# Earlier choice of slots and another order of loads for the first expert, in a kernel of linear attention and a mixture of experts

## The chip, the cores and the metric

The kernel runs on one core of one Trainium2 chip. The time is the device time of one execution in microseconds; several executions are timed and the median counts. A profile is taken of one further execution.

## The reference

The attention part keeps a 40 x 40 state for each of 4 x 8 heads and steps through 768 positions. Its output is the input of a mixture of 8 experts, of which each token uses the one with the largest logit.

```python
for t in range(S):                       # attention, B=4, H=8, S=768, D=40
    y[:, :, t] = einsum('bhd,bhde->bhe', rt, state)
    Sa = einsum('bhde,bhe->bhd', state, at)
    state = state * wt[:, :, None, :] - einsum('bhd,bhe->bhde', Sa, bt) \
            + einsum('bhd,bhe->bhde', vt, kt)
...
x = attn_out.transpose(0, 2, 1, 3).reshape(B * S, H * D)      # 3072 x 320
logits = x @ w_gate                      # experts, E=8, D=320, F=1024
e_idx = argmax(logits, axis=1)
...
for e in range(E):
    h = maximum(x[mask] @ w1[e], 0.0)
    out[mask] = gate_w[mask, None] * eom[mask, e, None] * (h @ w2[e])
```

## The kernel before

**Attention.** The positions are cut into 12 chunks of 64. In each chunk a triangular system has to be solved for 32 heads, 16 in each half (q = 0 and 1). `Att.run` writes out the order by hand as coroutines that yield after each step. A background coroutine prepares chunks (`prep`: loads, scans, masks on POOL, products pl on PE) and inverts the triangles of two chunks at once on DVE (`tinv`, with the tiles Tt, Ns, tmpf, and as its last step the transpose of line 350 into Tc). The chain from chunk to chunk is `crit`: five steps for each half, with matmuls into pa, evictions As on ACT (line 399), the copies XU (lines 438 and 439), and the state's step pS, tmS and XS. After each step of `crit` the background goes on by four steps (`RATE = 4`). `tail` computes the output of a half (VU, pM, the masked products M on DVE, pY) and ends in x on DVE (line 495), which `route` transposes (pxt) and multiplies by the gates into logits LG. When all inversions are written out, the pool of the preparation's tiles closes (`s.pre.close()`) and the background runs `Moe.early`; its pools stand on the other side of SBUF and take over this memory.

**Choice of slots.** `pick` takes the logits of several chunks at a time, as `NB` says: after chunk 3 chunks 0 to 3, after chunk 7 chunks 4 to 7, after chunk 10 chunks 8 to 10, after chunk 11 this one. It runs 18 small instructions on DVE, finds each token's place in its expert, and writes records into a table `tab` in DRAM with one indirect DMA from POOL for each half chunk (line 739), each of which waits for the one before. After chunk 7 (`HALF`) the first 240 places of each expert are all that the early work uses.

**The first expert.** `early` loads the weights of expert 0 through one staging tile st (4 KB a partition): three pieces of w1, three of w2. Each is loaded on SP's queue, cast on ACT to a rounded part (w1h, w2h; lines 767 and 774), and subtracted on DVE for the rest (w1l, w2l; lines 769 and 775). `slots` reads the table into tr (line 846) and turns it on DVE into tb (line 848) and ti (line 850); `tokens` gathers 240 tokens with two indirect DMAs (line 789) and transposes them into xh and xl. `expert` then computes eight blocks of the first layer (ph, line 820; 8 matmuls each here, then hh on ACT and hl on DVE), of which `early` runs the first `E0 = 4` inside the attention, and the second layer (po, lines 833 to 835), whose rows go out by indirect DMA. `experts` runs what is left when the attention's memory is free, beginning with the loads of expert 1.

The instructions of each engine are put in order by a planner, from the order in which they are written, their dependencies and its own estimate of durations. `issue_after(i)` keeps what is written under it behind instruction i on the engine of i.

Of the kernel before, what the change touches and what calls it, by code (L numbers as in the profile page):

```python
# [9 lines left out]
F32 = mybir.dt.float32  # L10
F32R = mybir.dt.float32r
# [4 lines left out]
ALU = mybir.AluOpType  # L16
# [578 lines left out]
E0 = 4  # L595


class Moe:
    def __init__(s, ctx, tc, ident, wg, wo, w1, w2, out):
        s.tc, s.nc, s.ident = tc, tc.nc, ident  # L600
# [50 lines left out]
        s.nc.sync.dma_start(out=s.tab.rearrange("(p n) f -> p n f", p=128), in_=s.t0)  # L651

    HALF, HT, half = 7, 2, False
    NB = {3: (0, 4), 7: (4, 4), 10: (8, 3), 11: (11, 1)}

    def route(s, c, q, x, pool, psx):

# [91 lines left out]
        V.tensor_reduce(out=out, in_=t, axis=AX.X, op=ALU.max)  # L749


    def weights(s, e, wp, sp):

        nc = s.nc
        w1h = wp.tile([128, 3, FF], F32R, name="w1h", tag="w1h")
        w1l = wp.tile([128, 2, FF], F32R, name="w1l", tag="w1l")
        w2h = wp.tile([128, 8, DM], F32R, name="w2h", tag="w2h")
        w2l = wp.tile([128, 8, DM], F32R, name="w2l", tag="w2l")
# [83 lines left out]
    def slots(s, pool):  # L842

        nc = s.nc
        tr = pool.tile([TS, 32, 4], F32, name="tr", tag="tr")
        nc.sync.dma_start(out=tr, in_=s.tab.rearrange("(t p) f -> p t f", p=TS))
        tb = pool.tile([TS, 4, 32], F32, name="tb", tag="tb")
        nc.vector.tensor_copy(out=tb, in_=tr.rearrange("p t f -> p f t"))
        ti = pool.tile([TS, 2, 32], I32, name="ti", tag="ti")
        nc.vector.tensor_copy(out=ti, in_=tb[:, 0:2])  # L850
        return tb, ti

    def early(s, ctx, psx):

        pool = lambda n, b: ctx.enter_context(s.tc.tile_pool(name=n, bufs=b, side="right"))
        s.wpa, s.tp0 = pool("wpa", 1), pool("tp0", 1)
        with s.tc.tile_pool(name="sp0", bufs=1, side="right") as sp:
            w = s.weights(0, s.wpa, sp)
            s.W0 = next(w)
            yield from w  # L860
        while not s.half:
            yield
        s.tabs = s.slots(s.tp0)
        t = s.tokens(s.tabs, 0, 0, 2, s.tp0, psx)
        T = next(t)
        next(t)
        for _ in range(30):
            yield
        yield from t
        s.hp0 = ExitStack()  # L870
        hp = s.hp0.enter_context(s.tc.tile_pool(name="hp0", bufs=E0, side="right"))
        s.hp = hp, TS * 2
        s.E0 = s.expert(2, s.W0, T, lambda: s.hp, lambda: s.ps1(), lambda: s.ps2())
        s.ps1 = lambda: psx(CAP)
        for _ in range(E0):
            next(s.E0)
            yield

    def experts(s, ctx):
        tc = s.tc  # L880
# [9 lines left out]
        def tok(tabs, *u):  # L890
            t = s.tokens(tabs, *u, tp, psx)
            T[u[:2]] = next(t)
            next(t)
            return t

        def wts(e):
            w = s.weights(e, s.wpa if e % 2 == 0 else wpb, sp)
            W[e] = next(w)
            return w

# [4 lines left out]
            for _ in prep:  # L905
                pass

        t = tok(s.tabs, 1, 0, 2)
        w = wts(1)
        tabs = s.slots(tp)  # L910
        t2 = tok(tabs, 0, 2, 2)
        unit(0, 0, 2, chain(w, t))
        s.hp0.close()
# [131 lines left out]
def rwkv_moe_kernel(tc, win, din, rl, vl, vt, r, k, v, w, a, b, wg, wo, w1, w2, out, nch=12):  # L1045
    nc = tc.nc
    with ExitStack() as ctx:
# [6 lines left out]
        with ExitStack() as c1:  # L1054
            with ExitStack() as c2:
                att = Att(c2, tc, ident, win, din, rl, vl, vt, nch=nch)
                moe.fill()
                ps = lambda sh, nm, tag="tl", n=3: lambda *_: att.ps.tile(sh, F32, name=nm, tag=tag, bufs=n)
                att.run(lambda c, q, x: moe.route(c, q, x, att.p2, ps([128, 4, 128], "pxt")),
                        moe.loads, lambda: moe.early(c1, lambda n: ps([128, 512], "px0", "pl", 2)()[:, 0:n]))  # L1060
# [45 lines left out]
```

## Time and profile before

| | us |
|---|---|
| median of 3 runs | 725.73 |
| lowest and highest run | 725.46, 727.76 |
| the profiled execution | 727.63 |
| its span in the profile | 725.9 |
| PE busy | 648.0 (89%) |
| DVE busy | 465.7 (64%) |
| ACT busy | 344.8 (47%) |
| POOL busy | 206.8 (28%) |

The span is the time between the first and the last instruction that the profile shows. The busy time is summed over the span. All times in the rows below count from the start of the span. PE is the matmul engine TensorE, DVE is VectorE, ACT is ScalarE, POOL is GpSimd, SP the engine that issues most DMAs.

### The profile page before, as it was taken

The numbers are of one execution on the slowest core, as the hardware profiler recorded it, in microseconds if no ns is written. First come the engines' busy times: TensorE is split into PE (matmuls) and PEld (weight loads), VectorE is DVE, ScalarE is ACT, GpSimd is POOL, SyncE is SP. The second block draws the span as 40 slices with busy tenths as digits, with TensorE's granted clock in tenths as the row PEclk, the third lists the DMA queues.
The fourth block names the chain that finished last, engine by engine and source line by source line (L and its number), as shares of the span: only waits on it lengthen the run. The fifth ranks groups of instructions, "written<-read, shape, count | busy, mean of one in ns | idle before, by whom it ended". The sixth has DMA issues, their size and how long they took to land.

```text
span 725.9 us, 21141 instructions
## 1 busy us (share of the span) xinstructions
PE 648.0 (89%) x8866; PEld 582.8 (80%) x8866; DVE 465.7 (64%) x904; ACT 344.8 (47%) x791; POOL 206.8 (28%) x316
## 2 busy tenths in 40 slices
PE   6766887899998899989999898779999999999993
PEld 6655776788887787887888788679999998898993
DVE  7694699648997994899289554353675445544230
ACT  4866642376387237835753354142563334333120
POOL 9632302123134036304112100334433142412111
PEclk9867998799998899999999989889999999999997
DMA  8785443157556365652325742085575433530000
GB/s 200 170 191 139 117 121 78 55 140 176 121 135 149 90 109 126 144 123 80 98 61 103 139 122 78 21 229 143 151 220 160 125 117 105 183 89 24 25 12 22
DMA packets 66007, 85.12 MB, mean 117 GB/s; under 512 B 34766, under 2 KB 51793, under 8 KB 65906
## 3 DMA queue, kind: packets, MB, share of 16 engines
q1 hardware_dynamic: 61976, 74.67, 41.6%
q0 software_dynamic: 3840, 8.91, 4.3%
q8 instruction: 72, 1.18, 0.7%
q14 instruction: 29, 0.24, 0.1%
q10 hardware_dynamic: 90, 0.13, 0.1%
HBM read 67.59 MB, written 8.96 MB: 105 GB/s over the span
## 4 chain that ended last, share of the span: by engine, by line
PE 49%; DVE 16%; issue 12%; DMA 10%; ACT 8%; POOL 1%; SPq 1%; POOLq 0%; ACTq 0%; DVEq 0%
PE ph L820 12%; PE pa L408 5%; PE po L835 4%; PE po L833 4%; PE po L834 4%; PE pM L480 4%; ACT N L250 4%; DVE tmpf L328 3%; PE pl L242 3%; PE pt L184 2%; DMA out_dram<-y,ti 2%; PE pY L493 2%; ACT LA L230 2%; PE pY L492 2%; PE pS L446 2%
## 5 line engine op out<-in xcount | busy, mean ns | idle before, releaser
L825 DVE SCALAR_TENSOR_TENSOR hl<-ph,hh 128x480 fp32r<-128x480 f32 (+1 forms) x76 | 41.9, 563 | 67.0 <-ACT hh L824 54.5
L820 PE MATMUL ph<-xh,w1h 128*128 128x480 f32 (+1 forms) x228 | 79.8, 354 | 2.5 <-DVE hl L825 1.3
L833 PE MATMUL po<-w2h,hh 128*120 128x320 f32 x256 | 79.0, 312 | 1.9 <-ACT hh L824 1.7
L820 PE MATMUL ph<-xl,w1h 128*128 128x480 f32 (+1 forms) x228 | 79.4, 351 | 0.0
L232 POOL TENSOR_SCALAR_AFFINE_SELECT LA<-LA 64x192 f32<-64x192 f32 x144 | 57.1, 428 | 75.1 <-ACT LA L230 73.9
L824 ACT ACTIVATE hh<-ph 128x480 fp32r<-128x480 f32 (+1 forms) x76 | 36.8, 497 | 87.3 <-PE ph L820 81.6
L834 PE MATMUL po<-w2l,hh 128*120 128x320 f32 x256 | 78.0, 308 | 0.0
L835 PE MATMUL po<-w2h,hl 128*120 128x320 f32 x256 | 75.7, 310 | 0.0
L838 POOL DMA_INDIRECT out_dram<-y,ti x32 | 33.7, 1054 | 139.7 <-DVE y L837 74.0
L242 PE MATMUL pl<-Am,kb 120*128 120x192 f32 (+1 forms) x288 | 63.3, 357 | 9.8 <-DMA Am<-Av 5.6
L399 ACT ACTIVATE As<-pa,hq 128x320 f32<-128x320 f32 x80 | 41.8, 528 | 54.6 <-PE pa L408 34.2
L250 ACT ACTIVATE N<-pl 32x384 f32<-32x384 f32 (+1 forms) x144 | 54.2, 376 | 23.8 <-PE pl L242 11.3
L739 POOL DMA_INDIRECT tab<-rec,si x24 | 27.7, 1153 | 119.4 <-DMA tab<-rec,si 48.3
L242 PEld LDWEIGHTS pl<-Am,kb 120*128 120x128 f32 x288 | 48.6, 212 | 13.6 <-ACT LA L230 5.2
L480 PE MATMUL pM<-R,VU 128*128 128x128 f32 x384 | 55.4, 300 | 3.6 <-ACT VU L472 3.5
L493 PE MATMUL pY<-KB,M 128*64 128x40 f32 x768 | 54.3, 230 | 1.0 <-DVE M L484 0.7
L480 PEld LDWEIGHTS pM<-R,VU 128*128 128x128 f32 x384 | 50.1, 209 | 5.4 <-ACT VU L472 4.5
L408 PE MATMUL pa<-As,Tc 64*32 64x40 f32 x1792 | 52.5, 209 | 1.7 <-ACT As L399 1.6
L492 PE MATMUL pY<-Sd,R 128*64 128x40 f32 x704 | 53.7, 232 | 0.0
L820 PE MATMUL ph<-xh,w1l 128*128 128x480 f32 (+1 forms) x152 | 53.4, 352 | 0.0
L408 PEld LDWEIGHTS pa<-As,Tc 64*32 64x32 f32 x1792 | 42.3, 116 | 10.6 <-issue 3.0
L493 PEld LDWEIGHTS pY<-KB,M 128*64 128x64 f32 x768 | 46.8, 138 | 4.3 <-issue 1.6
(183 smaller groups left out, 1542.2 us busy)
## 6 DMA issues: line engine op xcount, KB each, us to landing
kb<-in_din_dram SPq DMA_DIRECT2D x12, 720.0 KB
st<-in_w_dram SPq DMA_DIRECT2D x16, 512.0 KB
st<-in_w_dram SPq DMA_DIRECT2D x16, 480.0 KB
XS<-in_vt_dram SPq DMA_DIRECT2D x24, 256.0 KB
XU<-in_vt_dram SPq DMA_DIRECT2D x24, 256.0 KB
VU<-in_vl_dram SPq DMA_DIRECT2D x24, 208.0 KB
w<-in_win_dram SPq DMA_DIRECT2D x12, 371.2 KB
A<-in_din_dram SPq DMA_DIRECT2D x12, 360.0 KB
```

What stands on the lines that cost most here:

```text
L232: g.affine_select(out=la[:, :, i], in_=la[:, :, i], pattern=[[0, nj], [1, C]], base=0, channel_multiplier=-1, compare_op=ALU.is_gt, fill=0.0)
L242: s.mark['pl', c, side, g0] = nc.tensor.matmul(pl[:, i, 0:nj], KBt[:, 6 * side + g0 + i].rearrange("p n t -> p (n t)"), Am[:, g0 + i:g0 + ...
L250: s.mark['n', c] = nc.scalar.activation(out=nn, in_=pn, func=AF.Copy, scale=-1.0).ins
L408: nc.tensor.matmul(pa[o + w:o + w + 32, i], m(p)[o:o + 64], x[o:o + 64, i, :], start=start, stop=True, tile_position=(o, o + w), skip_grou ...
L480: nc.tensor.matmul(pM[:, i], VU[:, h0 + i].rearrange("p n t -> p (n t)"), R[:, :, h0 + i], start=True, stop=True)
L492: nc.tensor.matmul(o, R[:, side, i, :], Sd[:, i, :], start=True, stop=False)
L493: nc.tensor.matmul(o, Ms[i // 4][:, i % 4, side, :], KB[:, side, p, :], start=not c, stop=True)
L820: nc.tensor.matmul(ph, l, r, start=(i == 0), stop=(i == 7))
L825: nc.vector.scalar_tensor_tensor(out=b, in0=ph, scalar=0.0, in1=a.bitcast(F32), op0=ALU.max, op1=ALU.subtract)
L833: nc.tensor.matmul(po, hh[f][:, ts_], w2h[:, f], start=(f == 0), stop=False)
L834: nc.tensor.matmul(po, hh[f][:, ts_], w2l[:, f], start=False, stop=False)
L835: nc.tensor.matmul(po, hl[f][:, ts_], w2h[:, f], start=False, stop=(f == 7))
```

## The change

`NB` picks chunks 4 to 6 after chunk 6, and chunk 7 alone after chunk 7. `early` waits for the second of these first. Then two coroutines run side by side, step for step: `table` starts the read of the table, makes tb, ti and the gathers 48 steps later, and the transposes 14 steps after these; `first0` loads all of w1 of expert 0 into three staging tiles behind the read of the table, and casts them after 58, 3 and 3 steps. Then the memory of the staging tiles becomes that of w2h and w2l. `second0` loads w2 through a tile of the attention (LA) that is free by then, with two pieces under way at once, casts them after 14, 7 and 7 steps, and beside it four blocks of the first layer are run, one in three steps. `last` keeps an instruction behind all that is written before it on its engine. `slots` has become a coroutine; for the later experts it does what it did.

```diff
-    NB = {3: (0, 4), 7: (4, 4), 10: (8, 3), 11: (11, 1)}
+    NB = {3: (0, 4), 6: (4, 3), 7: (7, 1), 10: (8, 3), 11: (11, 1)}
...
+    def last(s, *engines):
+        pins = ExitStack()
+        for e in engines:
+            i = next((i for i in reversed(s.nc.cur_bb.bb.instructions) if i.engine == e), None)
+            if i is not None:
+                pins.enter_context(s.tc.issue_after(i))
+        return pins
...
+    def convert(s, h, l, raw):
+        nc = s.nc
+        r = slice(128 - l.partition_size(), 128)
+        with s.last(ACT, DVE):
+            nc.scalar.copy(out=h, in_=raw)
+            nc.vector.tensor_tensor(out=l, in0=raw[r], in1=h[r].bitcast(F32), op=ALU.subtract)
+
+    def first0(s, w1h, w1l, sp):
+        nc = s.nc
+        raw = [sp.tile([128, FF], F32, name="st", tag="st") for _ in range(3)]
+        for k in range(2):
+            with s.tc.issue_after(s.tr):
+                nc.sync.dma_start(out=raw[k], in_=s.w1[0, 128 * k:128 * k + 128])
+        for h in range(2):
+            nc.sync.dma_start(out=raw[2][64 * h:64 * h + 64], in_=s.w1[0, 256:320])
+        for k in range(3):
+            for _ in range(3 if k else 58):
+                yield
+            s.convert(w1h[:, k], w1l[:, k] if k < 2 else w1h[64:128, 2], raw[k])
+        yield
+
+    def second0(s, w2h, w2l, raw):
+        nc = s.nc
+        raw = raw.rearrange("p (i f) -> p i f", i=2)
+        parts = ((0, 3), (3, 3), (6, 2))
+        def fetch(i):
+            k, n = parts[i]
+            st = raw[:, i % 2, 0:n * DM].rearrange("p (k f) -> p k f", f=DM)
+            nc.sync.dma_start(out=st, in_=s.w2[0, 128 * k:128 * (k + n)].rearrange("(k p) f -> p k f", p=128))
+            return st
+        sts = [fetch(0), fetch(1)]
+        for i, (k, n) in enumerate(parts):
+            for _ in range(7 if i else 14):
+                yield
+            s.convert(w2h[:, k:k + n], w2l[:, k:k + n], sts[i])
+            if i == 0:
+                sts.append(fetch(2))
+        yield
...
-        nc.sync.dma_start(out=tr, in_=s.tab.rearrange("(t p) f -> p t f", p=TS))
+        s.tr = nc.sync.dma_start(out=tr, in_=s.tab.rearrange("(t p) f -> p t f", p=TS)).ins
...
+        yield tb, ti
+        with s.last(DVE) if pool is s.tp0 else ExitStack():
+            nc.vector.tensor_copy(out=tb, in_=tr.rearrange("p t f -> p f t"))
...
-        with s.tc.tile_pool(name="sp0", bufs=1, side="right") as sp:
-            w = s.weights(0, s.wpa, sp)
-            s.W0 = next(w)
-            yield from w
+    def table(s, psx):
+        sl = s.slots(s.tp0)
+        s.sl = next(sl)
+        for _ in range(48):
+            yield
+        next(sl, None)
+        t = s.tokens(s.sl, 0, 0, 2, s.tp0, psx)
+        s.T0 = next(t)
+        next(t)
+        for _ in range(14):
+            yield
+        for _ in range(3):
+            with s.last(PE):
+                next(t)
+            yield
...
         while not s.half:
             yield
...
+        with pool("sp0", 3) as sp:
+            w1 = s.first(wp1)
+            yield from both(s.table(psx), s.first0(*w1, sp))
+        wp2 = ctx.enter_context(pool("wpc", 1))
...
+        def units():
+            for _ in range(E0):
+                with s.last(PE):
+                    next(s.E0)
+                for _ in range(3):
+                    yield
+        yield from both(s.second0(*s.W0[2:], stage()), units())
```

## Rows read from the trace of the kernel before

**Rows 1.** Windows, expert stage: busy us (instructions) by engine, PE clock, DMA share, GB/s.
```profile
500.00:550.00 50.00, 50.00 (x361) 48.29 (x360) 30.63 (x51) 26.88 (x53) 22.28 (x21) 1.00 0.60 170
```

**Rows 2.** Windows of the stretch before 406 us, same columns.
```profile
355.00:360.00 5.00, 5.00 (x106) 4.45 (x104) 0.49 (x1) 3.72 (x10) 1.22 (x4) 1.00 0.08 25
...
375.00:380.00 5.00, 5.00 (x134) 4.67 (x132) 5.00 (x16) 0.44 (x1) 1.46 (x2) 1.00 0.22 46
```

**Rows 3.** Windows from 411 to 453 us, same columns.
```profile
411.00:413.00 2.00, 1.66 (x58) 1.44 (x54) 1.23 (x1) 1.14 (x3) 0.00 (x0) 1.00 0.75 48
413.00:415.30 2.30, 0.06 (x3) 0.00 (x0) 0.72 (x3) 1.23 (x3) 0.00 (x0) 1.00 0.99 227
415.30:420.00 4.70, 4.69 (x41) 4.03 (x41) 1.69 (x4) 2.03 (x4) 2.25 (x2) 0.66 0.52 164
420.00:425.00 5.00, 5.00 (x65) 4.36 (x64) 2.08 (x6) 1.73 (x4) 0.00 (x0) 0.63 0.60 156
...
430.00:435.00 5.00, 4.70 (x97) 4.17 (x97) 2.05 (x4) 2.93 (x6) 0.00 (x0) 1.00 0.47 157
...
440.00:445.00 5.00, 4.46 (x150) 4.11 (x148) 2.17 (x4) 1.84 (x4) 0.00 (x0) 1.00 0.49 122
445.00:450.00 5.00, 4.19 (x57) 3.63 (x57) 2.57 (x8) 2.71 (x9) 0.00 (x0) 1.00 0.16 58
450.00:453.30 3.30, 2.72 (x93) 2.44 (x94) 2.25 (x16) 2.21 (x7) 0.00 (x0) 1.00 0.02 5
```

**Rows 4.** Timeline of DVE: start us, us, engine, line, operation [idle before <-releaser].
```profile
404.11 1.97 DVE L350 STREAM_TRANSPOSE Tc<-Tt 128x1024 f32<-128x1024 f32 x1
...
414.58 0.27 DVE L848 COPY tb<-tr 120x128 f32<-120x128 f32 x1 [1.75 <-DMA tr<-tab]
414.77 0.48 DVE L495 TENSOR_TENSOR x<-pY,WT 128x320 f32<-128x320 f32 x1
```

**Rows 5.** Chain of waits around the table: start us, us, what.
```profile
404.32 4.29 DMA tab<-rec,si
408.63 5.93 DMA tr<-tab
...
483.79 3.94 DMA tr<-tab
```

**Rows 6.** Line 739, 340 to 410 us: ns min/median/max, first and last start.
```profile
L739 POOL DMA_INDIRECT tab<-rec,si x8: 969/992/1786, 377.0 to 404.3; - x8
```

**Rows 7.** Timeline of SP, the queue that issues loads.
```profile
406.14 0.35 SPq L763 DMA_DIRECT2D st<-in_w_dram  x1
...
409.09 2.44 SPq L373 DMA_DIRECT2D VU<-in_vl_dram  x1
...
471.81 0.81 SPq L763 DMA_DIRECT2D st<-in_w_dram  x2
```

**Rows 8.** Timeline of ACT.
```profile
412.86 0.42 ACT L438 COPY XU<-pa 64x320 f32<-64x320 f32 x1 [0.86 <-PE pa L408]
...
435.06 0.58 ACT L472 COPY VU<-ptU 128x512 f32<-128x512 f32 x1
...
476.53 1.05 ACT L767 CAST w1h<-st 128x1024 fp32r<-128x1024 f32 x1 [2.23 <-DMA st<-in_w_dram]
...
480.80 1.05 ACT L767 CAST w1h<-st 128x1024 fp32r<-128x1024 f32 x1 [0.93 <-DMA st<-in_w_dram]
```

**Rows 9.** Waits from 405 to 470 us: total us, times, longest.
```profile
ACT w2h L774 <- DMA st<-in_w_dram: 6.3, 3, 2.6
...
ACT w1h L767 <- DMA st<-in_w_dram: 2.4, 2, 1.8
```

**Rows 10.** Timeline of DVE: first and last of a pick, last of another.
```profile
367.86 0.20 DVE L693 TENSOR_REDUCE mem<-LG 128x8 f32<-128x64 f32 x1
...
376.06 0.18 DVE L736 RECIPROCAL rec<-mem 128x8 f32<-128x8 f32 x1
...
471.09 0.17 DVE L736 RECIPROCAL rec<-mem 128x2 f32<-128x2 f32 x1
```

More of the change, by code (lines that the diff above doesn't have):

```diff
@@ L595 @@
 E0 = 4
+PE, ACT, DVE = (getattr(mybir.EngineType, n) for n in ("PE", "Activation", "DVE"))
 class Moe:
@@ L749, in overfull, with first, second @@
         V.tensor_reduce(out=out, in_=t, axis=AX.X, op=ALU.max)
+    def last(s, *engines):
[5 more added lines that the diff above has]
+        return pins
+    def first(s, wp):
+        return [wp.tile([128, k, FF], F32R, name=n, tag=n) for n, k in (("w1h", 3), ("w1l", 2))]
+    def second(s, wp):
+        return [wp.tile([128, 8, DM], F32R, name=n, tag=n) for n in ("w2h", "w2l")]
@@ L752, in weights @@
     def weights(s, e, wp, sp):
         nc = s.nc
[L755 to L758, printed above, removed]
+        w1h, w1l = s.first(wp[0])
+        w2h, w2l = s.second(wp[1])
         yield w1h, w1l, w2h, w2l
@@ L850, in slots @@
         nc.vector.tensor_copy(out=ti, in_=tb[:, 0:2])
[L851 to L856, printed above, removed]
-        with s.tc.tile_pool(name="sp0", bufs=1, side="right") as sp:
-            w = s.weights(0, s.wpa, sp)
-            s.W0 = next(w)
-            yield from w
+    def table(s, psx):
[13 more added lines that the diff above has]
+            yield
@@ L861, in early, with both @@
+    def early(s, ctx, psx, stage):
+        pool = lambda n, b: s.tc.tile_pool(name=n, bufs=b, side="right")
+        wp1, s.tp0 = (ctx.enter_context(pool(n, 1)) for n in ("wpa", "tp0"))
+        def both(*gens):
+            gens = list(gens)
+            while gens:
+                for g in list(gens):
+                    if next(g, s) is s:
+                        gens.remove(g)
+                yield
         while not s.half:
             yield
-        s.tabs = s.slots(s.tp0)
-        t = s.tokens(s.tabs, 0, 0, 2, s.tp0, psx)
@@ L865, in early @@
[L865 to L869, printed above, removed]
+        with pool("sp0", 3) as sp:
+            w1 = s.first(wp1)
+            yield from both(s.table(psx), s.first0(*w1, sp))
+        wp2 = ctx.enter_context(pool("wpc", 1))
+        s.wpa = wp1, wp2
+        s.W0 = (*w1, *s.second(wp2))
         s.hp0 = ExitStack()
-        hp = s.hp0.enter_context(s.tc.tile_pool(name="hp0", bufs=E0, side="right"))
+        hp = s.hp0.enter_context(pool("hp0", E0))
@@ L872, in early @@
         s.hp = hp, TS * 2
-        s.E0 = s.expert(2, s.W0, T, lambda: s.hp, lambda: s.ps1(), lambda: s.ps2())
         s.ps1 = lambda: psx(CAP)
-        for _ in range(E0):
-            next(s.E0)
-            yield
+        s.E0 = s.expert(2, s.W0, s.T0, lambda: s.hp, lambda: s.ps1(), lambda: s.ps2())
+        def units():
[3 more added lines that the diff above has]
+                for _ in range(3):
+                    yield
+        yield from both(s.second0(*s.W0[2:], stage()), units())
@@ L896, in wts @@
         def wts(e):
-            w = s.weights(e, s.wpa if e % 2 == 0 else wpb, sp)
+            w = s.weights(e, s.wpa if e % 2 == 0 else (wpb, wpb), sp)
             W[e] = next(w)
@@ L906, in unit @@
                 pass
-        t = tok(s.tabs, 1, 0, 2)
+        t = tok(s.sl, 1, 0, 2)
         w = wts(1)
-        tabs = s.slots(tp)
+        sl = s.slots(tp)
+        tabs = next(sl)
+        next(sl, None)
         t2 = tok(tabs, 0, 2, 2)
@@ L1059, in rwkv_moe_kernel @@
                 att.run(lambda c, q, x: moe.route(c, q, x, att.p2, ps([128, 4, 128], "pxt")),
-                        moe.loads, lambda: moe.early(c1, lambda n: ps([128, 512], "px0", "pl", 2)()[:, 0:n]))
+                        moe.loads, lambda: moe.early(c1, lambda n: ps([128, 512], "px0", "pl", 2)()[:, 0:n],
+                                                    lambda: att.p5.tile([128, 2, NP, 66], F32, name="LA", bufs=4).rearrange("p a n t -> p (a n t)")))
                 att.range_bad(bad[0:120, 0:1])
```

1 line of the change is left out of this document (removed).

## The prediction, made before the changed kernel ran

> **What bounds the kernel now.** I read the windows first, stage by stage. From about 490 us on there is nothing to win for an edit of this kind: in the first expert stretch TensorE (PE) is busy 50.00 of 50 us at full clock [rows 1]. Before that the attention sets the pace, in three ways in turn. Up to 406 us it is VectorE (DVE): 5.00 of 5 us busy with the triangular inversion of chunks 10 and 11, after a hole around 355 to 360 where it does 0.49 of 5 us [rows 2]. The inversion ends with the transpose at 404.11 us that lasts 1.97 us, so at 406.08 [rows 4]; the first weight load leaves at 406.14 [rows 7], since it takes over the memory of the inversion's pool, which closes there. Everything the first expert prepares starts from this moment.
>
> After 406 the windows show what the stage loses [rows 3]. From 413 to 415.3 us PE is busy 0.06 of 2.3 us. Then it runs at a granted clock of 0.66 and 0.63 up to 425, a mix of its two levels of 1.2 and 2.4 GHz; before and after this the clock is 1.00. The reason for the hole stands on DVE [rows 4]: the copy of the slot table, tb, waits 1.75 us and starts at 414.58, and x of the attention, which the next PE work needs, stands behind it and starts at 414.77. Why tb is late stands in the chain of waits [rows 5]: the eighth table write (POOL, 404.32) takes 4.29 us to land, the table read tr leaves at 408.63 and takes 5.93 us. The eight writes run one after the other from 377.0 to 404.3 [rows 6], 27.3/7 = 3.9 us apart.
>
> The waits view names the other hold [rows 9]: ScalarE (ACT) stands 6.3 us in all before the three casts of the second layer's weights, 2.4 us before those of the first, each time for a load into the one staging tile; attention evictions queue behind them. What of this reaches PE between 430 and 453.3 us is its idle time there: 0.30 + 0.54 + 0.81 + 0.58 = 2.23 us [rows 3], the window that is left out (435 to 440) being full.
>
> **The change, part by part.** *The choice of slots.* One pick of eight columns becomes one of six, a chunk earlier, and one of two. DVE runs 18 instructions for a pick (plus the maximum with the bound). The old one is 18 at 0.14 to 0.23 us between 367.86 and 376.24, some 3.5 us; the one of two columns at the end of the attention is 18 at about 0.17 us, 3.1 us [rows 10]. The six-column pick I price like the eight-column one, 3.5 us. So DVE gets 3.5 + 3.1 - 3.5 = 3.1 us more in all, but in the full stretch after 365 us 0.4 us less. Two more exponentials on ACT (0.2 us each by the neighbours in size) are small; PE's 16 tiny matmuls and POOL's eight writes stay the same in number. Where the six-column pick lands the trace of before cannot show. At best the hole before 365 us takes it and the end of the inversion gains the 0.4 us; at worst all 3.1 us come before the inversion of chunks 10 and 11 and move its end. The hole is nearest: chunk 6 is routed a chunk before the pick at 367.86, and the hole has 4.5 us free in each 5 us. I take +0.3 us, range -0.4 to +3.1. POOL's six early writes fall among the masks of chunks 10 and 11, where POOL is busy 1.22 of 5 us; these masks are first read after the inversion, so waits of 3 to 4 us between writes cost nothing there.
>
> *The table.* Two writes instead of eight remain after chunk 7. At 3.9 us each from 377 they have landed by about 386. That gives 22 us of lead, but most of it is not used: tr, like the weight tiles, lies in the memory that comes free at 406.1. So tr leaves at 406.1 instead of 408.63, and now ahead of the weight loads. With the first load's bytes ahead it took 5.93 us; the second tr of the kernel took 3.94 [rows 5]. It lands at about 410.0 instead of 414.56, 4.5 us sooner, before x of chunk 9's second half needs DVE. The hole of 2.24 us goes. With it goes, I take it, the slow clock behind it: 4.7 x 0.34 + 5 x 0.37 = 3.4 us of full-speed time. The bounds are 0 (another hole of this length appears) and 5.6 us for both.
>
> *The first layer at once.* Four loads, 1.31 MB, are issued back to back behind tr; before, the next waited for the conversion of the last. The casts stand now 58 steps behind, at four steps per stage of the chain behind the third As of chunk 10's first half, then three and three steps on. ACT is there at about 410 to 413 (the XU copy that follows in the chain was at 412.86 [rows 8]). Expert 1 shows what four such loads need with no wait between them: issued at 471.81 [rows 7], its first cast began 4.7 us later, its third 9.0 us later, with loads of the second layer behind [rows 8]. From 406.5 this is 411.2 and 415.5, and 2 to 4 us more if tr goes first. So the casts still wait, in place of the 2.4 us of before. I take 1.5 us of new PE idle time, range 0 to 7. What would stand behind a waiting cast is the next As on ACT, and behind that the solves on PE. On SP the four loads go ahead of the attention's next VU load, issued at 409.09 [rows 7]; ACT writes into that tile at 435.06 [rows 8], so the burst, over by 420, costs it nothing.
>
> A rule speaks against just this. The Trainium skill (DMA: Bandwidth & Descriptors, section "Queues, rings and completion order") says that each DMA engine consumes descriptors in ring order; the two durations of tr, 5.93 us with a weight load ahead and 3.94 us, agree. By it the third piece would land only after the table and the 1 MB before it, and the sum would sit nearer the 7 us than the 1.5.
>
> *Layer two and the blocks.* The second layer's loads go to a free tile of the attention and are issued 14 steps, three to four stages, before their cast instead of one staging tile late. The four blocks of layer one (32 matmuls) run before them; their number and length don't change. What can be won is the 2.23 us of idle time; I take 1.5, range 0 to 2.2. The third piece still waits on SP for the first one's conversion, as before.
>
> *Behind the attention* nothing is edited. The next weight load follows the last reciprocal of the pick, 471.09 + 0.17 [rows 10], by half a microsecond at 471.81 [rows 7], and whatever the attention gains moves this start and all that comes after it.
>
> **The sum.** -2.24 (hole) - 3.4 (clock) + 1.5 (new casts) - 1.5 (layer two) + 0.3 (pick) = -5.3 us. The profiled execution took 727.63 us with a span of 725.9 us, 1.7 us around it; it becomes 722.3. It was 1.9 us slower than the median of the runs shown, 725.73, so for the median I forecast 720.4 and round to **720.5 us**. All bounds in favour give -2.24 - 3.4 - 2.2 - 0.4 - 0.34 (PE's idle time from 411 to 413) = -8.6 us, 717.1. What a measurement can tell here is 0.3%, 2.2 us.
>
> **The rivals.**
> 1. *The hole moves.* The casts, now three in a short stretch, or tb placed ahead of the mask products of the attention, make a hole of about the same length at 410 to 416, and the clock falls behind it as it did before. Then 2.24 and 3.4 us stay, and layer two's 1.5 us less 0.3 is all: 724.5, no difference that can be told. For it speaks that ACT is at the casts before the third piece can be there; against it that x no longer stands behind tr.
> 2. *The burst holds ACT longer: slower.* Place: the second and third cast, ahead of the As of chunk 10's second half. If the planner puts them directly behind the XU of the first half, ACT stands from about 413 until the last piece, 415.5 to 419.5, and casts for two more microseconds; from 411 to 413, while the table was read, the DMA engines were 0.75 busy and moved only 48 GB/s [rows 3]. With the clock loss kept, the time is 725.7 - 2.24 - 1.5 + 0.3 + W, W being PE's new idle time. It decides from W = 3.4 (even) on, and from W = 5.6 it is slower by over 0.3%; at W = 7, 729.3. Against it: ACT has other work that PE can be fed from, and the old casts waited with only 512 KB on the way.
> 3. *The extra pick is on the path.* All 3.1 us move the inversion's end: -5.3 + 2.8 = -2.5, 723.2. For it speaks DVE at 5.00 of 5 us; against it the hole before 365.
> 4. *More than the sum.* The chain of waits from 406 on runs free and its shorter steps also fill the idle time at the end of the attention: -8.6 or more, 716 to 717. PE's work of this stage stays, so not much beyond.
>
> **Chances.** The sum as worked out (717.5 to 723): 0.52. Rival 1: 0.21. Rival 2: 0.12. Rival 3: 0.07, half of it told as faster. Rival 4: 0.08. Faster by over 0.3% is 0.52 + 0.08 + 0.04 = 0.64; within 0.3% 0.21 + 0.03 = 0.24, slower 0.12. The range leaves out rival 2 and the far end of rival 4 and takes in rival 1: 716.5 to 725.5 us.
>
> **What would show it.** Right: tr is issued at about 406 and lands near 410; tb's wait on DVE is under 1 us; no window of 2 us with PE idle between 409 and 425, and clock 1.00 there; casts of the second layer without a wait for their load; the last reciprocal of the pick near 466. Wrong: tr leaves well before 406 (then memory did not hold it, and more is won), the inversion ends after 407 (the pick is on the path), casts of the first layer waiting 3 us or more in the middle of chunk 10, or a clock below 0.8 in any window from 410 to 430.

## The result: slower, 734.0 us

The changed kernel took 734.03 us (median of 4, 733.76 to 739.68). The kernel before took 726.75 beside it: the three runs shown ahead and a fourth of 733.18. The ratio is 1.0103, 95% interval [1.0057, 1.0149]. Its profiled execution took 734.26 us with a span of 732.5. The forecast was 720.5, range 716.5 to 725.5. Ratios, here and below, leave out runs that lie more than 1.5% above the fastest run of the same kernel; medians don't.

Read the loss from one series: the starts of x<-pY, the multiplication that ends each piece of the attention; x(c,q) is half q of chunk c. Up to x(6,1) the two kernels stay within 2.1 us of each other, and there the changed one is 1.1 us ahead. x(7,0) starts at 343.38 us before and 354.24 after, 10.9 late. The lateness is 12.8 at x(8,1), then shrinks: 7.5 at x(9,1), 6.2 at x(11,1), and the last choice of slots (the last reciprocal) starts at 477.24 in place of 471.09 [rows 10]. Nothing is won or lost behind that but 0.5 us.

The windows (columns as in [rows 1]), first of the kernel before where no row was shown yet:

```profile
330.00:340.00 10.00, 8.76 (x180) 7.81 (x180) 10.00 (x19) 5.03 (x12) 3.44 (x7) 1.00 0.27 75
340.00:350.00 10.00, 10.00 (x162) 8.33 (x160) 8.31 (x18) 9.03 (x26) 4.35 (x12) 1.00 0.39 119
370.00:380.00 10.00, 10.00 (x252) 9.26 (x250) 9.62 (x38) 4.00 (x10) 1.46 (x2) 1.00 0.22 51
380.00:390.00 10.00, 9.68 (x192) 8.52 (x189) 9.45 (x21) 2.92 (x7) 2.93 (x4) 1.00 0.53 85
```

and of the changed kernel:

```profile
330.00:340.00 10.00, 6.60 (x89) 5.74 (x88) 8.75 (x20) 4.41 (x12) 3.36 (x8) 0.67 0.20 64
340.00:350.00 10.00, 9.71 (x133) 8.36 (x133) 9.29 (x30) 8.07 (x23) 3.85 (x9) 0.82 0.20 69
370.00:380.00 10.00, 7.99 (x212) 7.15 (x211) 9.93 (x43) 5.55 (x16) 4.06 (x9) 1.00 0.92 191
380.00:390.00 10.00, 7.81 (x108) 7.22 (x107) 8.55 (x18) 0.72 (x2) 1.95 (x2) 0.66 0.10 22
410.00:415.00 5.00, 4.93 (x116) 4.34 (x113) 2.14 (x5) 1.85 (x4) 0.00 (x0) 1.00 1.08 278
415.00:420.00 5.00, 4.42 (x95) 4.01 (x94) 3.09 (x6) 1.69 (x4) 2.27 (x2) 1.00 0.97 209
420.00:425.00 5.00, 5.00 (x121) 4.48 (x122) 2.76 (x7) 3.11 (x7) 0.00 (x0) 1.00 0.59 148
450.00:460.00 10.00, 7.31 (x145) 6.55 (x144) 3.91 (x20) 3.81 (x10) 1.12 (x2) 0.81 0.10 35
```

PE idles at 330 to 340 and 370 to 390, where the prediction did not look, and the granted clock is 0.67 and 0.82 from 330 to 350 and 0.66 from 380 to 390; from 410 to 425, where it looked, PE is now busy 14.35 of 15 us at clock 1.00, and the hole of [rows 3] is gone. The longest wait of PE from 330 to 350 is 2.64 us for XS of the chain, until 333.60. What it would have had to do there, and what it did, shows in the timelines of PE, the kernel before first, then the changed one:

```profile
328.66 0.27 PE L470 MATMUL ptS<-ident,XS 64*128 64x64 f32 x1
...
332.16 2.05 PE L480 MATMUL pM<-R,VU 128*128 128x128 f32 x16
```

```profile
343.10 0.25 PE L707 MATMUL pxt<-mem,tri 128*128 128x48 bf16 x1
343.17 0.29 PE L709 MATMUL pxt<-mem,one 128*128 128x40 bf16 x5
343.40 0.37 PE L470 MATMUL ptS<-ident,XS 64*128 64x64 f32 x1
...
347.84 2.05 PE L480 MATMUL pM<-R,VU 128*128 128x128 f32 x16 [0.29 <-ACT VU L472]
```

L470 are the transposes that open the tail of piece (7,0). They ran at 328.66; now they run at 343.40, directly behind the first matmuls of pick (L707, L709). Why pick's matmul comes so late stands on DVE, in the changed kernel:

```profile
333.98 0.18 DVE L696 TENSOR_REDUCE mem<-LG 128x6 f32<-128x48 f32 x1
335.29 0.20 DVE L698 TENSOR_TENSOR mem<-LG,mem 128x48 f32<-128x48 f32 x1
336.60 0.20 DVE L700 SCALAR_TENSOR_TENSOR mem<-mem,wts 128x48 f32<-128x48 f32 x1
337.92 0.20 DVE L702 TENSOR_REDUCE mem<-mem 128x6 f32<-128x48 f32 x1
...
339.96 0.20 DVE L735 TENSOR_REDUCE mem<-mem 128x6 f32<-128x48 f32 x1 [1.25 <-ACT mem L728]
...
340.67 0.20 DVE L704 TENSOR_TENSOR mem<-mem 128x48 bf16<-128x48 f32 x1
```

The five steps of 0.2 us that pick's matmul waits for stretch from 333.98 to 340.87: between two of them stand two instructions of the inversion (1.1 us in all), and ahead of the fifth also a later step of pick (L735), for which DVE stood 1.25 us until ScalarE's exponentials were there. The last 2.2 us the matmul stands behind other work of PE. The code says why the tail waits with them: pick's sums lie in a tile of tag "tl", of which there are three, given out in the order written; the router's pxt and the tail's ptS, ptU, pM and pY take the same three.

The rest of what the prediction named, SP then DVE:

```profile
405.50 0.34 SPq L905 DMA_DIRECT2D tr<-tab  x1
405.89 2.42 SPq L784 DMA_DIRECT2D st<-in_w_dram  x2
```

```profile
415.20 0.26 DVE L910 COPY tb<-tr 120x128 f32<-120x128 f32 x1
```

tr leaves at 405.50 in place of 408.63 [rows 5], and tb waits for nothing where it waited 1.75 us [rows 4].

### The profile page after: what moved, and what is told of

Its sections match the earlier page's. It is cut to its first block, busy times and chain, and to the rows that moved or that the text cites. A ratio compares the mean times of both kernels' runs of the same rounds, so it can differ in the third digit from the quotient of the medians.

```text
span 732.5 us, 21165 instructions
## 1 busy us (share of the span) xinstructions
PE 649.1 (89%) x8866; PEld 585.5 (80%) x8866; DVE 469.2 (64%) x922; ACT 344.4 (47%) x793; POOL 209.4 (29%) x316
## 5 line engine op out<-in xcount | busy, mean ns | idle before, releaser
L232 POOL TENSOR_SCALAR_AFFINE_SELECT LA<-LA 64x192 f32<-64x192 f32 x144 | 60.2, 452 | 67.3 <-ACT LA L230 59.7
L242 PE MATMUL pl<-Am,kb 120*128 120x192 f32 (+1 forms) x288 | 65.0, 363 | 13.5 <-DMA Am<-Av 9.5
L897 POOL DMA_INDIRECT out_dram<-y,ti x32 | 35.3, 1104 | 137.3 <-DVE y L896 77.3
L480 PEld LDWEIGHTS pM<-R,VU 128*128 128x128 f32 x384 | 51.6, 214 | 8.6 <-ACT VU L472 7.7
L742 POOL DMA_INDIRECT tab<-rec,si x24 | 24.9, 1038 | 113.4 <-DVE rec L739 42.7
L848 POOL DMA_INDIRECT xg<-xd,ti x32 | 37.7, 1179 | 58.0 <-PE px L856 26.0
```

Of the source, the lines that this page charges most:

```text
L232: g.affine_select(out=la[:, :, i], in_=la[:, :, i], pattern=[[0, nj], [1, C]], base=0, channel_multiplier=-1, compare_op=ALU.is_gt, fill=0.0)
L242: s.mark['pl', c, side, g0] = nc.tensor.matmul(pl[:, i, 0:nj], KBt[:, 6 * side + g0 + i].rearrange("p n t -> p (n t)"), Am[:, g0 + i:g0 + ...
L480: nc.tensor.matmul(pM[:, i], VU[:, h0 + i].rearrange("p n t -> p (n t)"), R[:, :, h0 + i], start=True, stop=True)
```

## The experiments

The expectations call the theories by letters. Q, later T: what is written behind pick in the queue of the three tiles waits with it. Its rivals: pick's own DVE work (D, later V), GpSimd's six writes among its masks (P), and the new loads (F). Of these loads the first two fetches of w2 left at 370.84 and 372.07 in the changed kernel, 35 us ahead of w1, since their tile is free early.

**What costs the 11 us.** Four runs side by side, kernel before 727.16.

e1_old_pick, the changed kernel choosing as before:

```diff
-    NB = {3: (0, 4), 6: (4, 3), 7: (7, 1), 10: (8, 3), 11: (11, 1)}
+    NB = {3: (0, 4), 7: (4, 4), 10: (8, 3), 11: (11, 1)}
```

> The changed kernel with the old choice of slots: one pick of eight columns after chunk 7 again; loads, casts and blocks stay as changed. Theory Q (the early pick takes one of the three PSUM tiles that the attention's tails use, in the order written, so the tail of the first half of chunk 7 queues behind the pick's first matmul, which waits for DVE steps scattered in the inversion): the 11 us go and the gain after 406 us stays, 721 to 725 us; x of that half is back near 343. Rival D (it is only the 3 us of extra DVE work): 730 to 731. Rival P (six early table writes hold POOL): also 721 to 725, so this run alone does not tell P from Q. Rival F (the loss comes from the new loads): 732 to 734.

e2_split_only, the kernel before with this line of the change alone (the same diff the other way round).

> The kernel before with the split pick alone, nothing else changed. Q and P: x of the first half of chunk 7 is 10 us or more late, and with the old loads nothing is won after 406, so 733 to 739 us, slower than the changed kernel or equal to it. D: 729 to 730. F: 726 to 727, as before.

e3_pick_psum, the changed kernel with pick's sums in the unused end of the state's bank:

```diff
-            yield from s.pick(*s.NB[c], pool, psx().rearrange("p k t -> p (k t)"))
+            yield from s.pick(*s.NB[c], pool, s.pS()[:, 160:512])
```

> The changed kernel, with the sums of all picks in the unused end of the PSUM bank of the state product instead of one of the three tiles of the tails; the same instructions and the same DVE work. Q: the tails no longer queue behind a pick, x of the first half of chunk 7 is back near 343, and the time is 720 to 727 us. D, P and F: 732 to 735, unchanged.

e4_late_writes, the changed kernel with the six writes behind pick of chunk 7:

```diff
+        if c0 == 4:
+            return
-        for i in range(n):
+        for i in range(8 if c0 == 7 else 2 * c0, 2 * c0 + n):
```

> The changed kernel, with the six table writes of chunks 4 to 6 moved behind the pick of chunk 7, so that POOL has eight writes there as before the change; the split pick itself stays. P: 721 to 727. Q, D and F: 732 to 735, with x of the first half of chunk 7 still 10 us late.

Measured, with the ratio to the kernel before and its interval:

- e1_old_pick: 729.87, 1.0076 [1.0036, 1.0116]
- e2_split_only: 735.08, 1.0128 [1.0051, 1.0205]
- e3_pick_psum: 726.13, 0.9983 [0.9939, 1.0027]
- e4_late_writes: 731.51, 0.9984 [0.9925, 1.0044]; its ten runs spread from 721.03 to 738.82

More exact than times is one step within each trace, from x(6,1) to x(7,0). This step and the later milestones of all 20 profiles stand in this table, worked out from the starts in the traces (us). "Last choice" is the last reciprocal of pick, "second read" the second read of the table, and the last two columns are the distance from the last choice to this read and from this read to the end of the span:

```
kernel                    x(6,1)  last    second  read -  span -
                          -x(7,0) choice  read    choice  read
before                    15.7    471.09  483.79  12.7    242.1
after                     27.7    477.24  489.48  12.2    243.0
e1_old_pick               15.7    469.65  481.61  12.0    242.3
e2_split_only             27.4    479.24  490.78  11.5    241.9
e3_pick_psum              14.0    470.92  485.26  14.3    239.9
e4_late_writes            26.0    475.28  486.48  11.2    241.2
e5_pin_w2                 26.2    479.05  492.36  13.3    243.3
e6_before_psum            13.8    479.60  496.87  17.3    243.0
e11_psum_later            13.9    473.52  490.70  17.2    242.6
e12_psum_pin_later        14.0    467.19  482.63  15.4    242.9
f1_pick_4_later           16.5    469.90  482.79  12.9    242.8
f2_psum_later5            14.0    467.65  487.42  19.8    242.5
f3_psum_gate              14.0    474.15  489.56  15.4    242.3
f4_before_split_psum      13.9    482.76  502.82  20.1    242.3
h1_picks_6_10_later       16.5    465.46  488.16  22.7    239.0
h2_picks_6_7_10_later     16.5    463.79  487.09  23.3    242.2
h3_before_pick_10_later   15.7    470.97  494.72  23.8    241.7
i1_last_split_psum        14.0    466.55  479.71  13.2    243.3
i2_last_split_all_later   16.5    467.24  480.09  12.8    241.4
i4_last_split_later       16.5    476.02  488.98  13.0    241.6
```

The step is 26.0 to 27.7 us in the four kernels that have the new choice, begun at once and with its sums in the shared tiles, and 13.8 to 16.5 in all others. The split alone makes it (e2); the writes moved away leave it (e4); the same DVE work with its sums elsewhere doesn't have it (e3). For the 11 us at x(7,0), Q stands. The times are less clear. e1 misses Q's 721 to 725 and lies next to D's 730 to 731, though its step is that of the kernel before. e4's ratio is what P expected: what the six writes cost behind x(7,0) stays open. (The profiled executions of e11 and i4 were 6.6 and 4.7 us above their medians, so the times of their rows say little.)

**Where the expected gain is.** With the delay gone the gain should show, and doesn't: e3 is level with the kernel before. In its trace PE idles again at 415 to 417.4, and the waits view says for what (410 to 425 us of e3, then 405 to 430 us of e1):

```profile
PE px L857 <- DMA xg<-xd,ti: 2.3, 1, 2.3
```

```profile
PE px L856 <- DMA xg<-xd,ti: 4.6, 2, 3.4
```

These are the first tokens' transposes, pinned 14 steps behind their gather. In e1, the change without its choice, they cost PE 4.6 us. The next four runs (kernel before 722.51) try to mend this and two other guesses.

e5_pin_w2, the changed kernel with w2's fetches behind w1's last load:

```diff
-            nc.sync.dma_start(out=st, in_=s.w2[0, 128 * k:128 * (k + n)].rearrange("(k p) f -> p k f", p=128))
+            with s.tc.issue_after(s.w1last):
+                nc.sync.dma_start(out=st, in_=s.w2[0, 128 * k:128 * (k + n)].rearrange("(k p) f -> p k f", p=128))
```

> The changed kernel, with the first two fetches of w2 issued behind the last load of w1 (in the changed kernel they went out at 370.8 and 372.1 us, 35 us ahead of w1, since their stage is free early). Theory F: the two fetches fill the DMA engines at 370 to 379 (share 0.92 to 0.99) and PE's pause of 3.2 us at 379.0, which waits for nothing that the profile shows, comes from that: the pause goes, x(8,1) moves from 401.7 to about 399, and the time falls by 2 to 3 us to about 731. Rival N: the pause has another cause and stays; time 734, as for the changed kernel. The 11 us at x(7,0) stay by both, since pick is untouched.

Measured: 739.55, 1.0256 [1.0196, 1.0315]. This pause of PE, in the changed kernel's timeline, is gone,

```profile
382.19 0.29 PE L408 MATMUL pa<-As,Tc 64*32 64x40 f32 x2 [3.16 <-issue]
```

but one of 1.68 us ends at 418.20 now, where the fetches lie, the gather is waited for 3.2 us, and PE is busy 5.09 of 10 us from 415 to 425. The time is above that of both theories, F (731) and N (734).

e6_before_psum, the kernel before with e3's edit.

> The kernel before, with pick's sums in the spare end of the state's PSUM bank, no longer in one of the three tiles that the tail and the router share. Theory T (the tail of the piece just routed stands behind pick in that queue, and pick waits for steps scattered through a full VectorE): the kernel before pays this too at its picks of chunks 4 to 7 and 8 to 10 (first transposes of the tail 0.3 us behind pick's first matmul at 371.0 and 451.2), so x(8,0) and x(11,0) come earlier and the time falls by 2 to 6 us, to 721 to 725. Rival S: the queue is felt only where the split put the pick at chunk 6; the time stays at 726 to 727.

Measured: 747.43, 1.0368 [1.0320, 1.0416], against both expectations. The inversion ends 7.7 us earlier, but the eight writes don't: the first read leaves at 408.62 as before. DVE stands 3.95 us for it ahead of tb, PE is busy 2.22 of 5 us from 405 to 410, and x(9,1) starts 9.0 us later than before. By the table, another 4.6 us go between the last choice and the second read.

e11_psum_later, e3 with the transposes later:

```diff
-        for _ in range(14):
+        for _ in range(24):
```

> The changed kernel with pick's sums in the state's bank (726.1 us when run alone, with a hole at 415.0 to 417.4 in which PE waits for the gather of the first tokens, and a granted clock of 0.78 and 0.54 at 415 to 425), and the transposes of these tokens written 10 steps later (24 steps behind the gather in place of 14). Theory G: the hole is the pinned transposes waiting for the gather; written later, they wait for nothing, PE is busy through 410 to 425 at a granted clock of 1.00, and the time falls by the hole of 2.3 and by some 3.4 of clock (0.22 of 5 us and 0.46 of 5), to about 720.5. Rival H: the first layer's eight blocks are then written too late to end ahead of the last piece, and the work pushed behind takes back the gain: 724 to 727.

Measured: 728.36, 1.0057 [1.0017, 1.0098]. In its profile PE is full from 410 to 420, but idles 1.72 of 5 us behind that.

e12_psum_pin_later, e11 with e5's edit.

> All three: pick's sums in the state's bank, the first tokens' transposes 10 steps later, and the fetches of w2 behind w1. If theories G and F both hold: 718 to 720. If only G holds: about 720.5, as without the third edit. If the w2 fetches, now at about 410, lie on the gather (issued at about 409) and slow it, the transposes wait again and it is no better than 724.

Measured: 728.71, 1.0087 [1.0050, 1.0123], though its last choice is 3.9 us earlier than before. G fails in both runs, and e12 is "no better than 724" without the wait for the gather that was to be the reason. Where the 3.9 us went is answered further down.

Four more, kernel before 723.38.

f1_pick_4_later, the changed kernel with

```diff
         if q and c in s.NB:
+            for _ in range(4 if c in (6,) else 0):
+                yield
             yield from s.pick(*s.NB[c], pool, psx().rearrange("p k t -> p (k t)"))
```

> The changed kernel, with pick at chunk 6 begun 4 steps later in the order written; its sums stay in a tile that tails and router share. On PE it then stands behind the transposes of tail(7,0) and directly ahead of those of tail(7,1). Theory T (what is written behind pick in the queue of these three tiles waits with it): x(7,0) is no longer late (within 2 us of before, in place of 10.9 us late) and the delay appears one piece later, x(7,1) late by 5 to 11; time 729 to 734. Rival V (pick's VectorE work of some 3.5 us in the full inversion is what costs): x(7,0) and all behind it stay 10 us late, 734, since the same VectorE instructions are there.

Measured: 725.22, 1.0020 [0.9975, 1.0065], against 1.0103 without the two lines. Timeline of PE:

```profile
328.86 0.27 PE L470 MATMUL ptS<-ident,XS 64*128 64x64 f32 x1
...
332.37 2.05 PE L480 MATMUL pM<-R,VU 128*128 128x128 f32 x16
343.37 0.20 PE L709 MATMUL pxt<-mem,tri 128*128 128x48 bf16 x1
```

pick's matmul runs when it ran in the changed kernel, but the transposes of tail (7,0) are 14.5 us ahead of it. V is out, as the same DVE work is there. T is right on the cause, and its time (729 to 734) too high. The delay that was expected one piece later didn't come: x(7,1) is on time, as its tail was due only now (transposes at 344.90 in the kernel before, 343.60 here).

f2_psum_later5, as e11 with 19 steps.

> The changed kernel with pick's sums in the state's bank and the first tokens' transposes 5 steps later (19 behind the gather in place of 14; 24 gave 728 where the kernel before gave 722.5, with a wait of 4.4 us of these transposes for VectorE's xl). Theory G: 14 steps wait for the gather (2.3 us at 415), 24 push the first layer behind; 19 lie between and lose at neither end: 722 to 725 if before is at 727. Rival H: what is gained at 415 is lost behind 465 as work no longer left to fill the waits for the last table; no better than 726.

Measured: 730.41, 1.0089 [1.0046, 1.0133]. G fails again, and H's "no better than 726" holds: the last choice is 3.4 us earlier than before and the second read 3.6 later.

f3_psum_gate, e3 with w1's loads behind these copies out of the gathered tokens, and issued 50 steps later:

```diff
+        for k in range(3):
+            nc.gpsimd.tensor_copy(out=raw[k][0:1, 0:1], in_=s.xg[0:1, 1, 0:1])
```

> The changed kernel with pick's sums in the state's bank and the loads of w1 held until the first tokens' gather has landed (by three copies of one element on the otherwise idle GpSimd). Theory B: the gather lands 8 us behind its issue at 409.0 because the 768 KB of w1 fill the DMA engines at 408 to 415 (share 1.01); with them behind it, the table read and the gather land in 3 to 4 us each less time than with the burst ahead, the wait of 2.3 us at 415 goes, the clock stays at 1.00, and the time falls by 4 to 5 us below the 726 of pick's sums alone: 721 to 723. Rival C: the casts of w1 come 5 us later in turn and the first layer's blocks wait for these: the hole moves to 418 to 423, 726 or above.

Measured: 732.59, 1.0118 [1.0077, 1.0159]. The gather lands 2.4 us behind its last issue in place of 5.8, and ACT then stands for the load:

```profile
420.91 1.04 ACT L776 CAST w1h<-st 128x1024 fp32r<-128x1024 f32 x1 [6.09 <-DMA st<-in_w_dram]
421.86 0.58 ACT L473 COPY VU<-ptU 128x512 f32<-128x512 f32 x1
```

The cast waits 6.09 us, VU's copy is queued behind it, and PE waits 5.3 us for VU. C holds. (The loads of w1 are two of 512 KB and two of 256 KB, since the last 64 rows are loaded twice: 1.5 MB, not the 768 KB of the expectation.)

f4_before_split_psum, the kernel before with the new `NB` and e3's edit.

> The kernel before with two edits only: the split of the choice (chunks 4 to 6 once chunk 6 is routed, chunk 7 alone) and pick's sums in the state's bank; loads and first layer as in the kernel before. The split alone gave 735.1 (x(7,0) 8.9 late), the bank alone 747 where before was 722.5 (the table's eight writes end at 405 and PE waits 2.8 and 1.6 us of 5 at 405 to 415, since the inversion ended 7.7 earlier and the writes did not). Theory T plus W: the two edits need each other; with both, x(7,0) is in time, the writes end by 390, the table is read at 403, the hole at 413 moves earlier but is no longer than before; 722 to 727, that is 8 or more below the split alone and 15 or more below the bank alone. Rival: the moved loads and pins of the change carry the gain; then this one is at 730 or above.

Measured: 747.09, 1.0290 [1.0237, 1.0344]. The rival holds: without the moved loads and pins these two edits cost 2.9%; x(9,1) is 13.6 us late.

Three on the next pick (kernel before 726.17), each with f1's two lines for other chunks.

h1_picks_6_10_later, the changed kernel with `(6, 10)` in the place of `(6,)`.

> The changed kernel with pick begun 4 steps later at chunk 6 and at chunk 10 (at chunk 6 alone it was at 1.002 of the kernel before, the 10.9 us at x(7,0) gone). With chunk 6 alone, pick of chunk 10 still stood ahead of tail(11,0): PE waited 1.7 us at 450 for a copy of VU that stood on ScalarE behind pick's exponentials, and the granted clock was 0.50 at 450 to 455. Theory T2: the same coupling takes back the gain there; 4 steps later, pick(10) stands behind that tail, the wait and the clock loss of some 2.5 go, and the time falls by 2 to 4 us below chunk 6 alone, to 0.995 to 0.999 of before. Rival K: the stretch 440 to 495 is bound by the chain of the last pieces and the table behind them, and any gap filled in one place opens in another; 1.000 to 1.005.

Measured: 728.72, 1.0023 [0.9993, 1.0052].

h2_picks_6_7_10_later, with `(6, 7, 10)`.

> The same with pick of chunk 7 later too. Pick of chunk 7 leads to the table's last two writes (383 and 386 in the changed kernel), which have slack until the table is read at about 405: 4 steps later they end before 398, and nothing is lost. Theory T2: again up to 1 us better than with chunks 6 and 10 alone, as the tail behind pick(7) is freed. Rival K: the table is read later by the delay of pick(7) and the hole at 415 grows; 1.003 or more of before.

Measured: 731.60, 1.0049 [1.0018, 1.0080].

h3_before_pick_10_later, the kernel before with `(10,)`.

> The kernel before with one edit: pick of chunk 10 begun 4 steps later. Theory T2: the kernel before also has a tail directly behind pick at 451 (0.3 us behind its first matmul), and its granted clock is 0.90 and 0.76 at 460 to 480; placed behind the tail, the time falls by 2 to 4 us, to 0.995 to 0.997 of before. Rival K: nothing, since the chain of the last pieces sets the end there: 0.998 to 1.002.

Measured: 736.66, 1.0133 [1.0085, 1.0181].

T2 falls in all three; K has the times of h1 and h2, and not that of h3. The table shows why. In h1 and h2 the last choice comes 5.6 and 7.3 us earlier than before, and the end no earlier; in h3 it comes at the same time, and the end 10.5 us later. But the span always ends 239.0 to 243.3 us behind the second read of the table. That read waits for eight writes on GpSimd, none of which is issued before the last has landed. GpSimd in the kernel before, then in h2:

```profile
469.00 0.97 POOL L739 DMA_INDIRECT tab<-rec,si  x1 [1.40 <-DMA tab<-rec,si]
472.11 0.97 POOL L739 DMA_INDIRECT tab<-rec,si  x1 [2.14 <-DMA tab<-rec,si]
...
479.09 1.03 POOL L739 DMA_INDIRECT tab<-rec,si  x1 [3.16 <-DMA tab<-rec,si]
```

```profile
472.87 0.97 POOL L744 DMA_INDIRECT tab<-rec,si  x1 [4.93 <-DMA tab<-rec,si]
478.09 1.03 POOL L744 DMA_INDIRECT tab<-rec,si  x1 [0.30 <-issue]
484.91 1.00 POOL L744 DMA_INDIRECT tab<-rec,si  x1 [5.79 <-DMA tab<-rec,si]
```

Six are for chunks 8 to 10 and start when chunk 10 is chosen. Before, the sixth (469.00) is out just ahead of the last choice at 471.09. In h2 the last choice is at 463.79, but the sixth goes out at 472.87. In the 17 traces up to here the second read leaves 28.5 to 33.6 us behind the first of these writes (453.93 before, 453.98 in h2), while its distance from the last choice varies from 11.2 to 23.8. So the pick of chunk 10 sets the read as much as the last one does, and four steps later for this pick held the writes back. Writes also take longer once the next weights are loaded: in h2 the first five are 2.5 to 4.1 us apart, the last three follow at 5.2 to 6.8 us, with DMA shares of 0.80 to 0.97 from 465 to 480 and two gathers on GpSimd between the sixth and the seventh. How much of that is the loads was not tried.

The last three runs (kernel before 725.52) split that choice too:

```diff
-    NB = {3: (0, 4), 6: (4, 3), 7: (7, 1), 10: (8, 3), 11: (11, 1)}
+    NB = {3: (0, 4), 6: (4, 3), 7: (7, 1), 9: (8, 2), 10: (10, 1), 11: (11, 1)}
```

i1_last_split_psum, e12 with it.

> The changed kernel with pick's sums in the state's bank, the first transposes 10 steps later, the fetches of w2 behind w1, and the choice of chunks 8 to 10 split too (8 and 9 once chunk 9 is routed, 10 alone). Theory E: in all 17 profiles so far the span ends 239.0 to 243.3 us behind the issue of the second read of the table, and that read waits for eight writes that GpSimd makes one after the other, six of them only after chunk 10 is routed. Without the split this kernel had its last choice at 467.2, 3.9 earlier than before, but the last write waited for the six: the read went out 15.4 behind it, at 482.6, in place of 12.7. With only two writes left over, the read goes out 12 to 13 behind the last choice, at 480, and the time is 2 to 4 below before, 0.994 to 0.997. Rival L: the two last writes and the read are slow by themselves (loads of the next weights fill the DMA engines at 470 to 490), so the six cost nothing; no better than without the split, 1.000 to 1.009.

Measured: 721.01, 0.9941 [0.9909, 0.9974].

i2_last_split_all_later, h2 with it, the four steps for chunk 9 too.

> The changed kernel with pick begun 4 steps later at chunks 6, 7, 9 and 10, and the choice of chunks 8 to 10 split. Theory E: without the split this kernel had its last choice at 463.8 us, 7.3 earlier than before, and lost 10.6 of it since the read of the table went out 23.3 behind it (487.1). With four of the six writes done by 455, the read goes out 13 to 16 behind the last choice, at 477 to 480, and the time is 4 to 7 below before: 0.991 to 0.995. Rival L: the loads of weights make the last writes slow whatever stands ahead of them; 1.000 to 1.005.

Measured: 721.21, 0.9947 [0.9911, 0.9984].

i4_last_split_later, i2 without the steps for chunk 10.

> As the run before, but pick of chunk 10 not later: its two writes then start earlier, at about 450, and only the tail behind it waits, for a shorter pick of two columns. Theory E: the last choice at 464 to 467, the read 12 to 13 behind it, at 477 to 480: 0.991 to 0.996. Rival L: 1.000 to 1.005.

Measured: 727.70, 1.0034 [0.9999, 1.0069].

GpSimd in i2:

```profile
459.60 0.97 POOL L744 DMA_INDIRECT tab<-rec,si  x1 [1.41 <-DMA tab<-rec,si]
467.69 0.97 POOL L744 DMA_INDIRECT tab<-rec,si  x1 [7.12 <-DVE rec L741]
...
472.45 1.02 POOL L744 DMA_INDIRECT tab<-rec,si  x1 [0.94 <-DMA tab<-rec,si]
```

The seventh write waits for the choice alone, and the second read leaves 12.8 us behind the choice, where it was 23.3 in h2. E holds for i1 and i2: they are 0.6 and 0.5% faster than the kernel before, where the same kernels without the split were 0.9 and 0.5% slower than it. In i4 the time is L's and not E's. The read follows by 13.0 there too, but the last choice is late, at 476.02 in its one profile, with PE waiting 1.9 us for the VU of a tail behind pick of chunk 10. The cause of i4's loss stays open.

## Why the prediction was wrong

*The choice of slots* is the step that failed. It priced pick by its DVE work and by whether that moves the inversion's end. The price held: the inversion's last transpose starts at 403.41, 0.7 earlier (0.4 forecast), and rival 3 did not happen. The place did not. Pick was put into the hole at 355 to 360, and its steps ran from 333.98 to 348.41, where DVE was 10.00 and 8.31 of 10 us busy before. What the step left out is what stands behind pick in the tiles that it shares: +0.3 was forecast for the term, +10.9 came at x(7,0), made by the split alone in e2 and gone in e1, e3 and f1. What stands behind a waiting instruction was named for ACT and SP and not for PE, on which the wait fell.

*The table*: right in its place. tr left at 405.50 (406.1 forecast), tb waits for nothing (it starts at 415.20, 48 steps behind), the hole of 2.24 and the slow clock of 3.4 us are gone. Where tb does wait for tr, it starts 4.7 (e3) and 4.4 us (f1) behind its issue; 3.94 was taken. From x(8,1) to x(11,1) 6.6 of the 12.8 us come back. But e3 and f1 show that this is no gain of the early read alone: without the delay PE idles 2.41 (e3) and 1.69 us (f1) at 415 to 420, nearly all of it for the gather of the first tokens, and the times are level with the kernel before. The sum had no term for this gather. That in the changed kernel the delayed tails filled the stretch fits this and is argued, not tested. It is rival 1's end, 724.5, by the gather and not by casts or tb.

*New casts*: 1.5 forecast; PE waits 0.6 us in all from 395 to 450, for no cast. The casts of w1 start at 416.53, 421.11 and 428.96 (the first was forecast at 410 to 413) with no wait for a load, so the ring rule of the Trainium skill (DMA: Bandwidth & Descriptors, section "Queues, rings and completion order") was not put to the test. The four loads are 1.5 MB and not 1.31. Rival 2 named slower, by this burst; the sign came, its cause did not, though f3 shows the mechanism when the loads are late.

*Layer two*: the idle time did go, 1.67 us of it (PE 20.00 of 20 from 430 to 450, 18.33 before), but 0.89 came back at 450 to 460 (7.31 against 8.20). Its loads left at 370.84 and not 14 steps ahead of their cast, and PE's pause of 3.16 us at 379 stands behind them. With them moved (e5) this pause is gone.

*Behind the attention*: "whatever the attention gains moves all that comes after" is right only for the second read, not for the last choice that the step used. A last choice 5.3 us earlier, at 465.8, is worth its 5.3 us only if the pick of chunk 10 comes earlier by as much; with its writes where they are, the sixth (469.00) is not yet out. h1 and h2 had such a last choice with these writes no earlier, and lost the gain there; i1 and i2 have the last choice 4.5 and 3.9 us earlier than [rows 10] and kept 4.1 and 3.7 of it at the second read [rows 5].

The bound of 0.3% was too narrow as well: runs of the kernel before spread from 716.4 to 735.5 us over all measurements (one of 1933.69 aside), and its medians from 722.5 to 727.2.

## What to carry to other kernels

An operation that is cheap on its engine can be dear in a buffer: when one is moved, list which rotating tiles it takes, what takes the next one, and how long its own inputs trickle in through a full engine. Before adding up gains, find the last serial event that everything behind follows at a fixed distance (here a read, 239 to 243 us from the end in 20 of 20 profiles), and ask what else that event waits for. A gain that several edits must share is tested with the edits in pairs: the split, the other tiles and the moved loads were each worthless or harmful alone.

## What was not expected of the hardware

PE pauses that wait for nothing the profile shows ("issue") are rare here. From 330 us on the 20 traces have six of over 0.9 us, each where the DMA engines were busy or had just been: 3.16 us from 379 in the changed kernel (DMA share 0.92 from 370 to 380), 1.08 in e4 at 380 (0.79 from 370 to 380), 1.68 in e5 at 418, 1.72 in e11 at 422 and 1.06 in e12 at 418 (1.03, 1.03 and 1.08 from 415 to 420), 1.68 in f2 at 416 (1.03 from 410 to 415). The DMA view counts a queue of its own for instructions; in the changed kernel it has one packet in 372 to 382:

```profile
q1 hardware_dynamic: 1021, 1.70, 86.8%
q8 instruction: 1, 0.02, 0.8%
```

That PE waited for its instructions is argued, not shown: e3 and f1 have shares of 1.01 and 0.99 without such a pause, and in 11 of the 20 traces one of 1.6 to 2.7 us ends between 103 and 106 us, in the kernel before with the engines at 0.24 from 100 to 102 and 0.00 from 102 to 104.
